# Attention over pooled keys, then a gated MLP: three chunks pooled partly by VectorE, and a re-planned order

## The chip, the cores and the metric

One core of one Trainium2 chip. The metric is device time of one execution in microseconds, median of the runs; a profiled execution is taken beside them.

## The reference

Four batches, each with 12288 queries of 128 channels and a 384 x 32 image of 128 channels. The image is averaged over 4 x 4 pixels, which leaves 768 positions, and multiplied with `w_sr`; the result is both keys and values. Softmax attention follows, and the output goes row by row through an MLP of width 2048.

```python
kv_pool = kv.reshape(B, H // r, r, W // r, r, C).mean(axis=(2, 4))      # r = 4
k = v = kv_pool.reshape(B, -1, C) @ w_sr
s = (q @ k.transpose(0, 2, 1)) / np.sqrt(C)
a = np.exp(s - s.max(-1, keepdims=True)); a /= a.sum(-1, keepdims=True) + 1e-09
x = (a @ v).reshape(B * S, D)
h = x @ w_in
out = (h * (1.0 / (1.0 + np.exp(-1.702 * h)))) @ w_out
```

Inputs and output are float32; the kernel computes its matmuls in bf16.

## The kernel before

The 49152 rows are 96 groups of 512 rows. A group has 6 attention chunks (128 keys each) and 16 MLP chunks (128 of the 2048 hidden columns each). A chunk is *filled* (one 512-column matmul into a PSUM bank), goes through ScalarE (exponential L359, gated unit L619) into a slot of the SBUF tile `ag`, and is *drained*: four 129-column matmuls per attention chunk (L370, the 129th column sums the weights), one 512-column matmul per MLP chunk (L627). Fills are done two or three chunks at a time in banks 0 to 2 and 3 to 5; ScalarE takes such a fill as one instruction. Drains accumulate in the remaining banks (6 and 7; with two-chunk fills also 2 and 5), handed out by `acc()`, and VectorE evacuates them: L393 and L396 for attention, L638 for the MLP. Order of the work: attention of groups 0 to 47 (batches 0 and 1), their MLP, attention of groups 48 to 95, their MLP.

Some chunks bypass ScalarE: VectorE computes the exponential (`early_exp`) or the gated unit (`lent_gelu`) of the chunks in `rolling`, `lent` and `early`, one instruction at a time between its other work (`early_step`).

Every engine works through its instructions in order, and the kernel writes that order itself (`manual_schedule`): a planner at the end of the file keeps a clock `now` for TensorE, `dve` for VectorE and `end` for ScalarE in units of a 512-column matmul, and emits a fill, a drain or one of the `extras` by these. Its constants (`COST`, `COPY`, `SMALL`, `PAUSE` and so on) and the lists `sizes`, `first`, `SUM`, `rolling`, `lent` decide the order; semaphores then keep the data right on the chip.

**Keys.** For batches 0 and 1 the image is loaded in six chunks of 128 image rows by 16 pixels x 128 channels (a half of the image's columns). `load_chunk` issues them on GpSimd's DMA queue, which casts to bf16 on the way, into slots of the tile `x` that attention output will fill later. `pool_chunk` sums the pixels on TensorE: 16 matmuls with the pixel as the weights and `sum4` (128 x 32) as the moving operand (L141); L144 copies the result, and `key_and_value` makes keys and values (L163 to L166). Batch 1's loads are issued at groups 10 and 12 behind a `gate` (a VectorE and a GpSimd memset that hold the queue back until then), and their pooling at the groups in `SUM`. For batches 2 and 3 the sums are made by accumulating DMAs into `kvs` during the first MLP (`add_kv`, L175), `sum_kv` (L181), `put_pooled`, `turn_pooled` and `make_k`, each step some groups after the last (`background_moe`).

**Queries.** Groups 0 to 9 are loaded by casting DMAs on GpSimd's queue (`load_q`) and turned on TensorE (`transpose_q`, L244). Groups 6 and 7 share one load, `load_q(1, 2, 4)`, issued after the six chunks of batch 0. For 6 to 9 `later` puts the transposes in `extras` at the step in `first`. All others go through `cast_q`, a DRAM copy in bf16, and a transposing DMA on SP's queue (`load_qT`).

Of the kernel before, what the change touches and what calls it, by code (L numbers as in the profile page):

```python
# [24 lines left out]
def kernel(  # L25
    ctx, tc, q, kv, w_sr, moe_w_in, moe_w_out, out,
):
    nc = tc.nc
    B, N, C = q.shape
    _, H, W, _ = kv.shape  # L30
    r = 4
    Hp, Wp = H // r, W // r
    J = Hp * Wp
    JC = J // 128
    d_ff = moe_w_in.shape[1]
    FCH = d_ff // 128
    scale = 1.0 / (C ** 0.5)
    G = 512
    SG = 4 * G
    NG = B * N // G  # L40
    NS = NG // 4
    GB = NG // B
# [18 lines left out]
    R = 2  # L61
    XS = NS // R
    EARLY = 4
    AG = 102

    cpool = ctx.enter_context(tc.tile_pool(name="const", bufs=1))
# [46 lines left out]
    def x_tile(s):  # L113
        return x[:, s % XS * SG:(s % XS + 1) * SG]
# [2 lines left out]

    HC = H // 128
    h = J // 2
    kv_tiles, kv_sums, pooled, pTs, kTs, vs = {}, {}, {}, {}, {}, {}  # L120

    def new_keys(b):
        kTs[b] = kvres.tile([128, J], BF, name="kT")
# [4 lines left out]
    def load_chunk(b, jc):  # L128

        a, ch = divmod(jc, HC)  # L130
        t = x_tile(XS - 1 - jc)
        nc.gpsimd.dma_start(out=t, in_=kv_r[b, a, ch])
        kv_tiles[b, jc] = t.rearrange("p (wp w1 c) -> p w1 wp c", w1=r, c=C)

    def pool_chunk(b, jc):

        ps = acc()
        t = kv_tiles.pop((b, jc))
        for wp in (0, 2, 1, 3) if (b, jc) == (0, 0) else range(4):
            for w in range(r):  # L140
                nc.tensor.matmul(ps[:, 32 * wp:32 * wp + 32], t[:, w, wp, :], sum4,  # L141
                                 start=(w == 0), stop=(w == r - 1))
        pTs[b, jc] = kvtmp.tile([128, 128], BF, name="pTc", bufs=2)
        nc.vector.tensor_copy(pTs[b, jc], ps[:, 0:128])  # L144

# [24 lines left out]
    def add_kv(b, n):  # L170
        i, w = divmod(n, r)
        if n == 0:
            kv_sums[b] = kvsum.tile([Hp, 2, Wp, C], F32, name="kvs")
        for i2 in range(2):
            nc.gpsimd.dma_start(out=kv_sums[b][:, i2], in_=kv_p[b, i, w, :, i2],  # L175
                                **({"accum_op": ADD} if n else {}))
# [7 lines left out]
        nc.sync.dma_start(out=pool_bf[b, a].rearrange("w h c -> h w c"), in_=pooled[b, a])  # L184

    def turn_pooled(b, a):
        pTs[b, a] = kvtmp.tile([128, 1, h], BF, name="pT")
        nc.sync.dma_start_transpose(out=pTs[b, a], in_=pool_bf[b, a].rearrange("w h c -> (w h) c"))

    def put_k(b, a):  # L190
# [60 lines left out]

    first_f = x[:, 0:2 * SG].bitcast(F32)
    nc.sync.dma_start(out=first_f, in_=kv_r[0, 0, 0])
    w_sr_f = cpool.tile([128, C], F32)
    nc.sync.dma_start(out=w_sr_f, in_=w_sr)
    load_q(0, 0, 1)
    load_q(0, 1, 2)
# [22 lines left out]
    for m in range(0, 128, 32):  # L280
        p = slice(m, m + 32)
# [19 lines left out]
            nc.tensor.matmul(banks[:32, 2, :], ones, ones.unsqueeze(1).broadcast_to([128, 16, 32]),  # L301
                             start=True, stop=True)

    w_in_sb = cpool.tile([128, d_ff], BF)
    w_out_sb = cpool.tile([128, FCH, C], BF)

    ag = agpool.tile([128, AG, 512], BF, name="ag")
    warm(13)
# [26 lines left out]
        return K * len(free_frames())  # L335

    early = range(NG // R, NG // R + EARLY)
    rolling = [(i, JC - 1) for i in (31, 35, 45, 55, 56, 63, 64, 78, 91)]
    lent = [(g, FCH - 1) for g in (4, 6, 8, 9, 13, 15, 17, 53, 54, 56, 58, 60, 64, 65, 68, 69, 72, 73, 77, 81, 83, 85, 88, 91, 93)]
    turn = [("a",) + c for c in rolling if c[0] < early[0]] + [("m",) + c for c in lent if c[0] < early[0]]  # L340
    turn += [("a",) + c for c in rolling if c[0] > early[-1]] + [("m",) + c for c in lent if c[0] > early[-1]]
    aside = agpool.tile([128, K, 512], BF, name="aside")
# [10 lines left out]

    def fill_attn(chunks, ps):
        for k, (i, jc) in enumerate(chunks):
            rhs = qTs[i // 4][:, 0, (i % 4) * G:(i % 4 + 1) * G]
            nc.tensor.matmul(ps[:, k, :], kTs[i // GB][:, jc * 128:(jc + 1) * 128], rhs,  # L357
                             start=True, stop=True)
        nc.scalar.activation(place([("a",) + c for c in chunks]), ps, AF.Exp, scale=scale)  # L359
# [68 lines left out]
        raw = qpool.tile([128, 1, SG], BF, name="qT")[:, 0, 0:2 * G].bitcast(F32)  # L428

    def early_step():  # L430
        nonlocal steps
        on_dve(next(steps))
        if steps.gi_frame.f_locals["last"]:
            steps = None
            made[early_todo.pop(0)] = dve

    def early_exp(ps, out):
        last = False
# [49 lines left out]
        yield 3.5  # L488

    raw = None  # L490
    made, used = {}, []
    steps, early_todo = None, [c for c in rolling if c[0] < early[0]]
    early_todo += [c for c in lent if c[0] < early[0]]
    early_todo += [(i, jc) for i in early for jc in range(JC)]
# [38 lines left out]
        nc.gpsimd.memset(one, 0.0)  # L533

    TURN = {6: 3, 7: 4, 8: 5, 20: 6, 21: 7, 22: 8, 25: 9, 32: 10, 35: 11, 42: 12}
    SUM = {13: (0,), 14: (1,), 15: (2,), 17: (3,), 19: (4,), 22: (5,)}
    CAST = {0: [5], 13: [6], 14: [7], 15: [8], 16: [9], 26: [10, 11], 27: [12]}
    CAST_MOE = {20: 13, 21: 14, 22: 15, 23: 16, 33: 17, 34: 18, 35: 19, 36: 20, 37: 21, 38: 22, 39: 23}

    def background(i):  # L540

        first_round = i < GB * 2
        s = TURN.get(i, NS) if first_round else i // 4 + 3 if i % 4 == 0 else NS
        if s < NS:
            load_qT(s)
        if i == 5:
            load_rest(2, 2)
        if i in CAST:
            gate()
            for s in CAST[i]:  # L550
                cast_q(s)
        if i in (10, 12):
            gate()
            for jc in range(i % 10 * 3 // 2, i % 10 * 3 // 2 + 3):
                load_chunk(1, jc)
        for jc in SUM.get(i, ()):
            extras.extend([(pool_chunk, 1, jc), (key_and_value, 1, jc)])
        if i in (28, 33, 38):
            put_away(0, (i - 28) // 5)
        if i in (31, 36, 41):  # L560
            bring_back(0, (i - 31) // 5)
        if i == 40:
            new_raw()
        if i == 28:
            gate()
            nc.gpsimd.dma_start(out=w_in_sb, in_=moe_w_in)
        if i == 29:
            gate()
            nc.gpsimd.dma_start(out=w_out_sb, in_=moe_w_out.rearrange("(o p) c -> p o c", p=128))

    def background_moe(g):

        n, g = divmod(g, 4 * XS)
        m, odd = divmod(g - 9, 2)
        m += FIRST
        if n == 0 and FIRST <= m < RT // PART:
            (bring_back if odd else put_away)(n, m)
        g += n * 4 * XS
        nonlocal low, raw
        if g == 12:  # L580
            low = EARLY * JC
            order[:] = [f for f in order if f >= low // K]
        if g in CAST_MOE:
            gate()
            cast_q(CAST_MOE[g])
        if g in (41, 42):
            load_qT(g - 28)
        if g == 43:
            raw = None
            background(early[0])  # L590
        for b, lo in ((2, 0), (3, 24)):
            if lo <= g < lo + 8:
                gate()
                add_kv(b, g - lo)
            for a in range(2):
                step = g - lo - 9 - a
                if step == 0:
                    sum_kv(b, a)
                    on_dve(3.5)
                    put_pooled(b, a)  # L600
                if step == 2:
                    turn_pooled(b, a)
                if step == 4:
                    extras.append((make_k, b, a))
# [63 lines left out]


    NA, NM = NG * JC, NG * FCH  # L670
    chunks, sizes = [], [1] * 2 + [2] * 26
    chunks += [(0, 0), (1, 0), (0, 1), (1, 1)]
    chunks += [(i, jc) for i in range(2, 6) for jc in range(2)]
    chunks += [(i, jc) for jc in range(2, JC) for i in range(6)]
# [57 lines left out]
    def prepare(p):  # L732
# [3 lines left out]
        for i, jc in part:  # L736
# [20 lines left out]
        12: [(pool_chunk, 0, 4)],  # L757
        13: [(key_and_value, 0, 4)],
        15: [(pool_chunk, 0, 5)],
        16: [(key_and_value, 0, 5), (later, 6)],  # L760
        17: [(later, 7)],
        18: [(later, 8), (later, 9)]}

    FIXED, CHUNK, SWITCH, HANDOVER, EVACUATE = 0.295, 1.978, 6.0, 1.0, 4.5
    COST = {pool_chunk: (1.9, 2.6), key_chunk: (0.3, 2.4), value_chunk: (0.3, 2.4),
            transpose_q: (1.05, 4.2), early_fill: (1.0, 5.5), key_and_value: (0.55, 3.5),
            make_k: (0.8, 3.2)}  # L770
    COPY = {pool_chunk: 1.5, key_chunk: 1.5, value_chunk: 1.5, key_and_value: 2.8, transpose_q: 3.2}
    SMALL = 0.26
    RECIPROCAL = 8.2
    PAUSE = 1.0
    end, extra_at = [], 0.0
    source, dve = None, 0.0
    early_left = 2 * (G // T) * EARLY
# [1 line left out]
    def on_dve(cost):  # L779
        nonlocal dve  # L780
        dve = max(dve, now + 1.0) + cost
# [36 lines left out]
    for n in range(len(seq)):  # L818
        fill(n + 2)
        jobs(n + 3)  # L820
        while True:
# [3 lines left out]
            f = None  # L825
            if extras and now >= max(extra_at, bank):
                f, *args = extras[0]
            if steps and dve <= now + 3.0:
                early_step()
            near = todo and todo[0][0] == "m" and todo[0][2] > 10  # L830
# [4 lines left out]
            if f:  # L835
                now = max(now, bank) + COST[f][0]
                f(*args)
                free[last_acc] = dve + 1.0 if f is early_fill else copied(f)
                if f is make_k:
                    on_dve(2.5)  # L840
                extra_at = max(now + PAUSE, dve + 1.5 if f is make_k else 0.0)
                if f is early_fill:
                    pass
                else:
                    extras.pop(0)
                continue
# [67 lines left out]
```

## Time and profile before

| What | us |
|---|---|
| median of 3 runs (lowest, highest) | 946.6 (946.47, 946.94) |
| profiled execution, device time | 946.45 |
| its span in the profile | 944.7 |
| TensorE matmuls busy | 938.5 |
| ScalarE busy | 930.5 |
| VectorE busy | 655.5 |
| GpSimd busy | 66.7 |

PE is TensorE's matmuls, PEld its weight loads, DVE VectorE, ACT ScalarE, POOL GpSimd, SP the engine that issues most DMAs. Times inside the profile count from the span's start. Ends of matmuls are modelled, so starts are compared where gaps matter. The granted clock of TensorE was 1.0 throughout. The two attention stages lie at about 8 to 160 us and 483 to 640 us.

### The profile page before, as it was taken

What the parts mean: (1) busy time and instruction counts of PE and PEld (TensorE: products, weight loads), DVE (VectorE), ACT (ScalarE), POOL (GpSimd) and SP (SyncE); (2) the same over time, 40 slices, a digit from 0 to 9 for tenths busy, and PEclk for the clock granted to TensorE, in tenths of its full rate; (3) what the DMA queues carried; (4) which work ended last, traced back from release to release, by engine and by line L of the source; (5) the groups of instructions that cost most, each with busy time, mean ns of one, the idle gap of its engine ahead of it and who ended that gap; (6) DMA issues with size and microseconds to landing.
All of it is one profiled execution on the core that took longest, in us unless ns stands there. A gap on an engine that the chain in (4) does not pass through costs nothing.

```text
span 944.7 us, 15547 instructions
## 1 busy us (share of the span) xinstructions
PE 938.5 (99%) x6278; PEld 500.9 (53%) x6278; DVE 655.5 (69%) x1202; ACT 930.5 (98%) x706; POOL 66.7 (7%) x115
## 2 busy tenths in 40 slices
PE   9999999999999999999999999999999999999998
PEld 4777776444444444445446777744444444444444
DVE  5547565896878789878757645458777986386681
ACT  6999999999999999999999999999999999999997
POOL 3101003310000332000000000000000000000000
PEclk9999999999999999999999999999999999999999
DMA  9998947996877899664435683652222221212222
GB/s 210 206 196 176 189 90 102 145 134 139 167 151 115 123 144 130 116 111 93 63 63 117 131 157 91 116 124 41 38 38 41 37 42 34 44 34 45 34 45 45
DMA packets 380456, 97.30 MB, mean 103 GB/s; under 512 B 354560, under 2 KB 377984, under 8 KB 379904
## 3 DMA queue, kind: packets, MB, share of 16 engines
q1 hardware_dynamic: 351840, 64.19, 36.9%
q0 software_dynamic: 28272, 31.99, 22.3%
q8 instruction: 49, 0.80, 0.4%
q14 instruction: 23, 0.19, 0.1%
q10 hardware_dynamic: 272, 0.13, 0.0%
HBM read 52.49 MB, written 49.81 MB: 108 GB/s over the span
## 4 chain that ended last, share of the span: by engine, by line
PE 98%; DMA 1%; ACT 0%; DVE 0%; POOL 0%; issue 0%; POOLq 0%
PE banks L627 35%; PE banks L617 35%; PE banks L370 14%; PE banks L357 12%; PE banks L422 1%; DMA x<-in_kv_dram 1%; PE banks L416 1%; PE banks L141 0%; ACT ag L359 0%; PE banks L655 0%; POOL x L230 0%; PE banks L163 0%; PE banks L301 0%; PE banks L244 0%; PE banks L203 0%
## 5 line engine op out<-in xcount | busy, mean ns | idle before, releaser
L619 ACT ACTIVATE ag<-banks 128x1536 bf16<-128x1536 f32 (+1 forms) x507 | 677.7, 1468 | 0.0
L617 PE MATMUL banks<-x,w_in_sb 128*128 128x512 bf16 x1511 | 408.8, 379 | 0.0
L627 PE MATMUL banks<-ag,w_out_sb 128*128 128x512 bf16 x1495 | 405.2, 379 | 0.0
L359 ACT ACTIVATE ag<-banks 128x1536 bf16<-128x1536 f32 (+2 forms) x191 | 245.9, 1410 | 3.3 <-PE banks L357 2.9
L627 PEld LDWEIGHTS <-w_out_sb 128*128 128x128 bf16 x1520 | 148.5, 98 | 178.2
L617 PEld LDWEIGHTS <-w_in_sb 128*128 128x128 bf16 x1511 | 146.5, 98 | 170.6 <-issue 0.5
L370 PEld LDWEIGHTS <-ag 128*128 128x128 bf16 x2268 | 145.7, 98 | 44.3 <-issue 0.5
L370 PE MATMUL banks<-v,ag 128*128 128x129 bf16 x2268 | 163.6, 220 | 0.1
L357 PE MATMUL banks<-qT,kT 128*128 128x512 bf16 x543 | 148.4, 379 | 1.3 <-DVE kT L165 0.4
L638 DVE STREAM_TRANSPOSE o_sb<-banks 128x512 f32<-128x512 f32 x95 | 67.3, 708 | 79.8 <-PE banks L627 79.0
L453 DVE SCALAR_TENSOR_TENSOR ea<-ea,eb 128x512 f32<-128x512 f32 x132 | 90.5, 686 | 4.1 <-DVE ea L453 0.6
L393 DVE RECIPROCAL rec<-banks 128x3 f32<-128x3 f32 x124 | 22.2, 179 | 92.7 <-PE banks L370 92.2
L484 DVE RECIPROCAL eb<-ea 128x256 f32<-128x256 f32 x50 | 84.9, 1726 | 0.9
L396 DVE TENSOR_TENSOR x<-banks,rec 128x384 bf16<-128x384 f32 x124 | 69.1, 557 | 4.3
L477 DVE SCALAR_TENSOR_TENSOR ea<-ea,eb 128x512 f32<-128x512 f32 x100 | 68.3, 683 | 2.7
L357 PEld LDWEIGHTS <-kT 128*128 128x128 bf16 x543 | 45.9, 98 | 26.0 <-issue 1.4
L175 POOL DMA_DIRECT2D kvs<-in_kv_dram x32 | 40.7, 1338 | 20.8 <-DMA kvs<-in_kv_dram 17.5
L442 DVE TENSOR_SCALAR ea<-banks 128x512 f32<-128x512 f32 x33 | 22.8, 692 | 26.0 <-PE banks L422 25.7
L464 DVE TENSOR_SCALAR qT<-banks 128x512 f32<-128x512 f32 x25 | 17.3, 692 | 34.0 <-PE banks L416 34.0
L533 POOL MEMSET gate_tile<- 1x1 f32 x38 | 3.6, 94 | 320.4 <-DVE gate_tile L532 315.1
L448 DVE SCALAR_TENSOR_TENSOR eb<-eb,ea 128x512 f32<-128x512 f32 x33 | 22.8, 691 | 0.9
L472 DVE SCALAR_TENSOR_TENSOR eb<-eb,ea 128x512 f32<-128x512 f32 x25 | 17.3, 692 | 0.9
(78 smaller groups left out, 316.7 us busy)
## 6 DMA issues: line engine op xcount, KB each, us to landing
out_dram<-o_sb SPq DMA_DIRECT2D x380, 64.0 KB, 1.9
kvs<-in_kv_dram POOLq DMA_DIRECT2D x32, 384.0 KB, 6.4
q_bf<-in_q_dram POOLq DMA_DIRECT2D x21, 512.0 KB, 7.0
x_bf<-x SPq DMA_DIRECT2D x13, 768.0 KB, 5.6
x<-in_kv_dram POOLq DMA_DIRECT2D x11, 512.0 KB, 10.2
x_bf<-x SPq DMA_DIRECT2D x6, 384.0 KB, 4.7
x<-in_kv_dram SPq DMA_DIRECT2D x1, 1024.0 KB, 5.1
x<-in_q_dram POOLq DMA_DIRECT2D x4, 256.0 KB, 12.1
```

The costliest lines, as they stand in the source:

```text
L175: nc.gpsimd.dma_start(out=kv_sums[b][:, i2], in_=kv_p[b, i, w, :, i2], **({"accum_op": ADD} if n else {}))
L357: nc.tensor.matmul(ps[:, k, :], kTs[i // GB][:, jc * 128:(jc + 1) * 128], rhs, start=True, stop=True)
L359: nc.scalar.activation(place([("a",) + c for c in chunks]), ps, AF.Exp, scale=scale)
L370: nc.tensor.matmul(av_of[u][:, k * (C + 1):(k + 1) * (C + 1)], weights(("a", i, jc))[:, o:o + T], vs[i // GB][:, jc, 0:C + 1], start=(jc = ...
L396: nc.vector.tensor_tensor(to, ps[:, :, 0:C], rec.unsqueeze(2).broadcast_to([128, TS, C]), MUL)
L453: nc.vector.scalar_tensor_tensor(a, a, COEFFS[k], b, ADD, MUL)
L477: nc.vector.scalar_tensor_tensor(a, a, COEFFS[k], b, ADD, MUL)
L484: nc.vector.reciprocal(b[:, m:m + 256], a[:, m:m + 256])
L617: nc.tensor.matmul(ps[:, k, :], w_in_sb[:, fc * 128:(fc + 1) * 128], x[:, g % (4 * XS) * G:(g % (4 * XS) + 1) * G], start=True, stop=True)
L619: nc.scalar.activation(place([("m",) + c for c in chunks]), ps, AF.Gelu_apprx_sigmoid)
L627: nc.tensor.matmul(o_of[g], w_out_sb[:, fc, :], weights(("m", g, fc)), start=(fc == 0), stop=(fc == FCH - 1))
L638: nc.vector.transpose(o_sb, o_of.pop(g))
```

## The change

- Chunks 1, 3 and 4 of batch 1 (`ADDED`) are loaded as float32, without the cast, into memory that is free at that time: `kvs`, the tile of both MLP weights, and two slots of `x`. `kvs` also takes the place of the float32 copy of `w_sr`.
- `add_row` adds the four pixels of a row on VectorE, in three instructions, the last one giving bf16; `pool_added` then needs 4 matmuls in place of 16.
- Planner constants, `rolling`, `lent`, `SUM` and `first` get other values: two-chunk fills go on for 47 fills in place of 26, the transposes of groups 6 to 9 come at other steps, `lent` has 26 chunks in place of 25.
- The second half of the sums of batches 2 and 3 comes one group later, and turned keys get two buffers.

Across the whole program TensorE has 36 matmuls fewer, ScalarE six instructions more.

```diff
+    ADDED = (1, 3, 4)
...
+    kvs = kvsum.tile([128, 2, Wp, C], F32, name="kvs")
+    w_both = cpool.tile([128, 2 * d_ff], BF, name="w_both")
+    homes = [kvs.rearrange("p a w c -> p (a w c)"), w_both.bitcast(F32)]
+    homes += [x[:, s * SG:(s + 2) * SG].bitcast(F32) for s in (XS - 6, XS - 4, XS - 2)]
+    wide = dict(zip(ADDED, homes))
+    plain = [jc for jc in range(JC) if jc not in wide]
+    spots = {jc: XS - 1 - (JC if len(wide) == JC - 1 else k) for k, jc in enumerate(plain)}
...
-        t = x_tile(XS - 1 - jc)
+        if b and jc in wide:
+            nc.gpsimd.dma_start(out=wide[jc], in_=kv_r[b, a, ch])
+            return
+        t = x_tile(spots[jc] if b else XS - 1 - jc)
...
+    def add_row(jc):
+
+        last, wp = False, None
+        t = wide[jc].rearrange("p (wp e) -> p wp e", wp=r)
+        narrow_sum = wide[jc].bitcast(BF).rearrange("p (wp e) -> p wp e", wp=r)[:, :, 4 * C:5 * C]
+        for m in (0, 2):
+            nc.vector.tensor_tensor(t[:, m:m + 2, 0:2 * C], t[:, m:m + 2, 0:2 * C], t[:, m:m + 2, 2 * C:4 * C], ADD)
+            yield 3.2
+        nc.vector.tensor_tensor(narrow_sum, t[:, :, 0:C], t[:, :, C:2 * C], ADD)
+        added[jc] = narrow_sum
+        extras.extend([(pool_added, 1, jc), (key_and_value, 1, jc)])
+        last = True
+        yield 3.3
+
+    def pool_added(b, jc):
+
+        ps = acc()
+        t = added.pop(jc)
+        for wp in range(r):
+            nc.tensor.matmul(ps[:, 32 * wp:32 * wp + 32], t[:, wp, :], sum4, start=True, stop=True)
         pTs[b, jc] = kvtmp.tile([128, 128], BF, name="pTc", bufs=2)
         nc.vector.tensor_copy(pTs[b, jc], ps[:, 0:128])
...
-        pTs[b, a] = kvtmp.tile([128, 1, h], BF, name="pT")
+        pTs[b, a] = kvtmp.tile([128, 1, h], BF, name="pT", bufs=2)
...
-    w_sr_f = cpool.tile([128, C], F32)
+    w_sr_f = kvs[:, 0, 0, :]
...
-    rolling = [(i, JC - 1) for i in (31, 35, 45, 55, 56, 63, 64, 78, 91)]
-    lent = [(g, FCH - 1) for g in (4, 6, 8, 9, 13, 15, 17, 53, 54, 56, 58, 60, 64, 65, 68, 69, 72, 73, 77, 81, 83, 85, 88, 91, 93)]
+    rolling = [(i, JC - 1) for i in (33, 36, 45, 53, 56, 62, 76, 89, 92)]
+    lent = [(g, FCH - 1) for g in (6, 7, 10, 13, 14, 17, 52, 53, 55, 58, 59, 62, 63, 67, 68, 71, 73, 75, 77, 78, 82, 83, 86, 88, 91, 92)]
...
-    SUM = {13: (0,), 14: (1,), 15: (2,), 17: (3,), 19: (4,), 22: (5,)}
+    SUM = {13: (0,), 14: (1,), 15: (2,), 17: (3,), 21: (4,), 22: (5,)}
...
         for jc in SUM.get(i, ()):
-            extras.extend([(pool_chunk, 1, jc), (key_and_value, 1, jc)])
+            if jc in wide:
+                sums.append(add_row(jc))
+            else:
+                extras.extend([(pool_chunk, 1, jc), (key_and_value, 1, jc)])
...
-                step = g - lo - 9 - a
+                step = g - lo - 9 - 2 * a
...
-    chunks, sizes = [], [1] * 2 + [2] * 26
+    chunks, sizes = [], [1] * 2 + [2] * 47
...
         15: [(pool_chunk, 0, 5)],
-        16: [(key_and_value, 0, 5), (later, 6)],
-        17: [(later, 7)],
-        18: [(later, 8), (later, 9)]}
+        14: [(later, 6)],
+        15: [(pool_chunk, 0, 5), (later, 7)],
+        16: [(key_and_value, 0, 5)],
+        17: [(later, 8)],
+        26: [(later, 9)]}
...
-    COST = {pool_chunk: (1.9, 2.6), key_chunk: (0.3, 2.4), value_chunk: (0.3, 2.4),
+    COST = {pool_chunk: (2.1, 2.6), pool_added: (0.55, 2.6), key_chunk: (0.3, 2.4), value_chunk: (0.3, 2.4),
...
-    COPY = {pool_chunk: 1.5, key_chunk: 1.5, value_chunk: 1.5, key_and_value: 2.8, transpose_q: 3.2}
-    SMALL = 0.26
+    COPY = {pool_chunk: 1.5, pool_added: 1.5, key_chunk: 1.5, value_chunk: 1.5, key_and_value: 2.8, transpose_q: 3.2, make_k: 2.9}
+    SMALL = 0.2647
...
-    PAUSE = 1.0
+    PAUSE = 2.0
...
+            if sums and not steps:
+                steps = sums.pop(0)
             if steps and dve <= now + 3.0:
                 early_step()
...
-                if f is make_k:
-                    on_dve(2.5)
```

The key 15 stands twice in `first` after the change; the second one, with both entries, counts.

More of the change, by code (lines that the diff above doesn't have):

```diff
@@ L119 @@
     h = J // 2
-    kv_tiles, kv_sums, pooled, pTs, kTs, vs = {}, {}, {}, {}, {}, {}
+    kv_tiles, kv_sums, pooled, pTs, kTs, vs, added = {}, {}, {}, {}, {}, {}, {}
+    kvs = kvsum.tile([128, 2, Wp, C], F32, name="kvs")
[5 more added lines that the diff above has]
+    spots = {jc: XS - 1 - (JC if len(wide) == JC - 1 else k) for k, jc in enumerate(plain)}
     def new_keys(b):
@@ L142, in pool_chunk @@
                                  start=(w == 0), stop=(w == r - 1))
+        pTs[b, jc] = kvtmp.tile([128, 128], BF, name="pTc", bufs=2)
+        nc.vector.tensor_copy(pTs[b, jc], ps[:, 0:128])
+    def add_row(jc):
[15 more added lines that the diff above has]
+            nc.tensor.matmul(ps[:, 32 * wp:32 * wp + 32], t[:, wp, :], sum4, start=True, stop=True)
         pTs[b, jc] = kvtmp.tile([128, 128], BF, name="pTc", bufs=2)
@@ L172, in add_kv @@
         if n == 0:
-            kv_sums[b] = kvsum.tile([Hp, 2, Wp, C], F32, name="kvs")
+            kv_sums[b] = kvs[0:Hp]
         for i2 in range(2):
@@ L302, in warm @@
                              start=True, stop=True)
-    w_in_sb = cpool.tile([128, d_ff], BF)
-    w_out_sb = cpool.tile([128, FCH, C], BF)
+    w_in_sb = w_both[:, 0:d_ff]
+    w_out_sb = w_both[:, d_ff:2 * d_ff].rearrange("p (o c) -> p o c", c=C)
     ag = agpool.tile([128, AG, 512], BF, name="ag")
@@ L355, in fill_attn @@
         for k, (i, jc) in enumerate(chunks):
+            assert i < GB or (i // GB, jc) in vs
             rhs = qTs[i // 4][:, 0, (i % 4) * G:(i % 4 + 1) * G]
@@ L430, in early_step @@
     def early_step():
-        nonlocal steps
+        nonlocal steps, extra_at
         on_dve(next(steps))
         if steps.gi_frame.f_locals["last"]:
+            if "wp" in steps.gi_frame.f_locals:
+                extra_at = max(extra_at, dve + 1.0)
+            else:
+                made[early_todo.pop(0)] = dve
             steps = None
-            made[early_todo.pop(0)] = dve
     def early_exp(ps, out):
@@ L490 @@
     raw = None
-    made, used = {}, []
+    made, used, sums = {}, [], []
     steps, early_todo = None, [c for c in rolling if c[0] < early[0]]
@@ L556, in background @@
         for jc in SUM.get(i, ()):
-            extras.extend([(pool_chunk, 1, jc), (key_and_value, 1, jc)])
+            if jc in wide:
+                sums.append(add_row(jc))
+            else:
+                extras.extend([(pool_chunk, 1, jc), (key_and_value, 1, jc)])
         if i in (28, 33, 38):
```

## The prediction

> **What bounds the kernel now.** The page was read first: busy shares, then the chain that ended last.
>
> ```profile
> PE 938.5 (99%) x6278; PEld 500.9 (53%) x6278; DVE 655.5 (69%) x1202; ACT 930.5 (98%) x706; POOL 66.7 (7%) x115
> PE 98%; DMA 1%; ACT 0%; DVE 0%; POOL 0%; issue 0%; POOLq 0%
> ```
>
> The first row is each engine's busy us, share and instructions; the second, the chain's shares. TensorE and ScalarE both look full, but the chain runs over TensorE alone. A modelled busy share hides short gaps, so I took the starts of all 6278 matmuls from the trace. Back to back, a 512-column matmul takes 216 ns, one of 128 or 129 columns 56, of 32 columns 25. Against these floors TensorE loses only 7.2 us from its first matmul (0.97 us) to its last (940.95 us): 3.0 before 12.5 us, 3.5 from there to 65.4 us, 0.7 in the other 875. So the time is a sum of matmuls, plus waits in the first 65 us. ScalarE starts a three-chunk exponential every 1.33 us at best and averages 1.35: there is about 1% of slack, and ScalarE does not set the end. VectorE is free a third of the time. The windows by stage say the same: the start, then chunks of batch 1, then the steady second stage.
>
> ```profile
> 12.00:27.00 15.00, 13.93 (x164) 8.56 (x163) 9.03 (x24) 14.49 (x16) 1.56 (x4) 1.00 1.13 223
> 27.00:47.00 20.00, 20.00 (x224) 14.50 (x223) 11.26 (x34) 20.00 (x19) 3.48 (x10) 1.00 1.10 199
> 47.00:77.00 30.00, 29.88 (x387) 21.70 (x386) 13.23 (x49) 30.00 (x23) 2.17 (x7) 1.00 1.01 194
> ```
>
> The columns are busy us of TensorE, weight loads, VectorE, ScalarE and GpSimd, then granted clock (1.00), DMA share and GB/s. Only the start has TensorE below full, and there DMA is saturated (share above 1).
>
> **What is removed.** Three chunks are pooled by 4 matmuls in place of 16: 36 fewer. A window on one pooling shows the price.
>
> ```profile
> 20.59:20.99 0.40, 0.40 (x17) 0.40 (x17) 0.33 (x1) 0.40 (x2) 0.00 (x0) 1.00 1.06 215
> ```
>
> The group of its weight loads lists 96 ns for one:
>
> ```profile
> L141 PEld LDWEIGHTS <-x 128*128 128x128 bf16 x192 | 6.3, 96 | 4.2 <-DMA x<-in_kv_dram 1.4 <-DVE x L291 0.8 <-issue 0.2
> ```
>
> Sixteen matmuls and their loads take 0.40 us, 25 ns a pair: the loads overlap. 36 x 25 ns = 0.90 us, all on the path: **-0.9**. Laying the rows at these intervals along both instruction orders gives 930.04 us of TensorE work before and 929.14 after; the rest of its program is the same work in another order.
>
> The Trainium skill ("TensorE: Matmul & The Clock Gate", LDWEIGHTS) puts a 128-column weight load at columns / 1.2, some 107 ns; by that, 36 would save an estimated 3.8 us. The windowed row, with 25 ns, disagrees.
>
> **What is added off the path.** Each wide chunk has two adds over 512 elements per partition and a third over 512 with a bf16 result. Nearest row: L181, 676 ns for 96x512. 9 x 0.68 = 6.1 us of VectorE, spread over 20 us where it now works about half the time (11.26 of 20.00, 13.23 of 30.00). In the new order they stand between the drains' reciprocal and multiply (0.18 + 0.56 us a drain); from the first add to the pooled copy after it, VectorE has 4.6 us of work for 5.2 us of TensorE's. Cover is the spare accumulator banks: four while fills are two chunks wide, two later, each about 1 us of drain. I take 0; if the cover fails, one add, 0.7 us, per chunk, at most 2.
>
> Two-chunk fills go on for 21 fills more, in place of 14 of three: 21 x 904 - 14 x 1330 ns = +0.4 us of ScalarE (starts 904 and 1330 ns apart when back to back). One more second-matmul chunk goes to VectorE (-0.44 us of ScalarE, about 11 us of VectorE in a stage where it is busy 31 of 40). With ScalarE's 1% of slack: 0 on the path.
>
> Second buffer for turned keys, the second half of the sums one group later: VectorE's wait of 3.7 us at L181 goes, of which nobody waited on TensorE (two of its gaps there, 0.1 each): 0. On SP the second half's DMAs (put_pooled, turn_pooled, put_k, turn_k) move past one group's four output DMAs; three output buffers cover 20 us. 0. The changed constants only order the emission.
>
> **The loads.** Chunks 1, 3 and 4 now write 1 MB each instead of 0.5, from GpSimd's queue, and the chunks behind them and the four casts of q queue behind those. Before, successive casting loads landed 2.3 to 2.5 us apart (45.41, 47.69, 50.13 us). No row shows an uncast 1 MB load on this queue. Low bound: the same, as both read 1 MB. High bound: kvs loads of 384 KB f32, which land 1.5 us apart when quiet and up to 3.4 us when busy, 4 to 9 us per MB. I take 2.45: its source reads are the same and its rows as long, where the kvs rows have 512-byte pieces. Then, with the wait of the next part, the loads start near 41.6 us; chunk 0 lands near 47.3 (5.7 us, as before) and is pooled near 48.9, chunk 1 lands near 49.7 and VectorE reaches its add near 52.0, chunk 3 near 54.6 for 59.2: 0.
>
> **The transposes of raw q, moved forward: the one wait on the path.** The new order puts group 6's transposes (L244) ahead of chunk 5's pooling, group 7's just behind it. Their data is one cast load, issued at 7.56 us.
>
> ```profile
> 7.56 0.70 POOL L230 DMA_DIRECT2D x<-in_q_dram  x1
> ```
>
> From issue to landing:
>
> ```profile
> x<-in_q_dram POOLq DMA_DIRECT2D x1, 256.0 KB, 16.8
> ```
>
> And TensorE's timeline of before around its use (start, us, line, tiles, count, and idle time with its releaser):
>
> ```profile
> 19.65 0.67 PE L370 MATMUL banks<-v,ag 128*128 128x129 bf16 x9
> ...
> 23.57 0.56 PE L141 MATMUL banks<-sum,x 128*128 128x32 bf16 x16
> ...
> 24.61 0.39 PE L244 MATMUL banks<-ident,x 128*128 128x128 bf16 x4
> ...
> 26.88 0.59 PE L357 MATMUL banks<-qT,kT 128*128 128x512 bf16 x2 [0.23 <-ACT ag L359]
> ```
>
> The load lands at 24.31 us, at the saturated queues' pace (neighbours at 23.05 and 25.55), and its transposes begin at 24.61, so it was just in time. Up to the drain at 19.65 the two orders are alike. From there the changed one has, before group 6, six fills (1.30 us), 15 drains (0.84), 16 pooling (0.40) and two key/value matmuls (0.11): 2.65 us, and about 0.3 of waits like those of before (chunk 4 lands at 20.52). It arrives at 22.6 us and waits until 24.36: **+1.75**. Queued behind are drains, fills and chunk 5's pooling; ScalarE, without a fill, idles about 1.6 us.
>
> What that wait swallows: between 24.61 and 77 us TensorE of before waited 1.6 us (0.40 at 26.4 for ScalarE, 0.33 at 33 to 36, 0.27 at 48.9, 0.18 at 65, small ones). Those for ScalarE come back, as ScalarE is delayed too: I keep 0.35 around 28 us, 0.2 in the two-chunk stretch and 0.4 at the passage to three. So **-0.65** (between 0 and -1.6). After 77 us: unchanged.
>
> Sum: -0.90 + 1.75 - 0.65 = +0.2 us. The profiled execution took 946.45 us (span 944.7), 0.15 below the median of 946.6. So 946.65 for it, **946.8 us** for the median. This kernel's measurement tells about 0.2% (1.9 us) from no change.
>
> **The rivals.**
>
> *Slower, by late wide loads.* If an uncast load takes over about 4.7 us, chunk 1 comes later than VectorE reaches its add, and everything behind it on VectorE's queue waits: drains' evacuations, so banks, so TensorE. At the busy kvs price (8 us) VectorE waits 3.3 us for chunk 1 and 6.6 for chunk 3; less about 2.5 and 2 us that the banks cover, TensorE loses 0.8 + 4.6: 952 us. For it: DMA share is 1.0 to 1.1 there. Against: 4 us when quiet, and longer rows. 0.13. Other late copies, banks or chains on VectorE in the new order, each under 1 us but adding to over 2: 0.15, 948.5 to 950.
>
> The Trainium skill ("DMA: Bandwidth & Descriptors", Where 436 GB/s comes from) caps the SBUF side at 435 GB/s, an estimated 2.4 us per MB, so uncast would land like cast; no run yet shows it.
>
> *Faster, because weight loads are exposed.* If each removed pair costs its listed load, 96 ns, 36 save 3.5 us, not 0.9: 944.2. Against it, the sixteen in 0.40 us. 0.04. It is what the Trainium skill's rule on loads above would bring.
>
> *Faster, because the early wait absorbs more.* All 1.6 us of old waits vanish, and two or three later ones: -0.9 + 1.75 - 2.7 = -1.9 at the very best, 944.7. For it: no wait after 77 us matters. Against: ScalarE is starved by the same wait. 0.06.
>
> **How the numbers follow.** No measurable change 0.62 (own range 945.3 to 948.4), faster 0.10, slower 0.28. The range reaches from -1.3 (all old waits gone) to +2.5 or so (two adds uncovered plus one lost bank): 945.3 to 949.2; it leaves out the late loads at full price and the exposed weight loads.
>
> **What would show it.** Right: a wait of 1.5 to 2 us at L244's transposes ending near 24.4 us, TensorE full after it, pooling of wide chunks in 0.10 us, no wait on VectorE for wide chunks. Wrong: group 6's data landing before 23 us (then about 945), VectorE waiting for DMA at the adds, or TensorE gaps after 80 us above 1 us.

## The result, and the profile after

The changed kernel takes 949.16 us (949.02 to 949.36), the kernel before in the same comparison 946.76 (946.47 to 947.05): ratio 1.0026, 95% interval 1.0017 to 1.0034. That is 2.4 us slower, where 946.8 was forecast; it lies just inside the stated range, whose top was 949.2. The profiled execution took 949.02 us with a span of 947.2, against 946.45 and 944.7.

The page of the changed kernel, busy shares and the chain that ended last:

```profile
PE 932.2 (98%) x6128; PEld 500.5 (53%) x6242; DVE 667.4 (70%) x1226; ACT 929.3 (98%) x712; POOL 66.7 (7%) x115
PE 94%; DMA 2%; ACT 2%; issue 1%; DVE 0%; POOL 0%; POOLq 0%
```

TensorE's matmul count is 150 lower, but its weight loads, 36 fewer, tell the change: 114 matmul records are missing from this trace, which also lowers the busy time. The chain now holds DMA and ScalarE with 2% each, where DMA had 1% and ScalarE 0%. The windows of the first stages show where TensorE is less busy (TensorE, weight loads, VectorE, ScalarE, GpSimd, clock, DMA share, GB/s):

```profile
12.00:27.00 15.00, 12.05 (x147) 7.41 (x149) 8.09 (x22) 13.15 (x14) 1.56 (x4) 1.00 1.13 223
27.00:47.00 20.00, 19.51 (x220) 14.48 (x224) 11.27 (x34) 19.83 (x23) 2.60 (x7) 1.00 1.03 175
47.00:77.00 30.00, 29.47 (x349) 21.53 (x354) 18.41 (x58) 30.00 (x27) 3.13 (x10) 1.00 1.01 255
```

The first window falls from 13.93 to 12.05 us. Missing records lower these sums too (220 matmuls to 224 loads in the second row, 349 to 354 in the third), so the waits are read from starts below. TensorE's timeline in the first window names the wait:

```profile
20.48 0.56 PE L152 MATMUL banks<-sum,x 128*128 128x32 bf16 x16
...
21.61 0.50 PE L405 MATMUL banks<-v,ag 128*128 128x129 bf16 x6
22.15 0.39 PE L392 MATMUL banks<-qT,kT 128*128 128x512 bf16 x1
24.26 0.40 PE L278 MATMUL banks<-ident,x 128*128 128x128 bf16 x4 [1.72 <-DMA x<-in_q_dram]
...
26.90 0.60 PE L392 MATMUL banks<-qT,kT 128*128 128x512 bf16 x2 [0.31 <-DVE kT L199]
...
28.62 0.59 PE L392 MATMUL banks<-qT,kT 128*128 128x512 bf16 x2 [0.33 <-ACT ag L394]
```

Group 6's transposes (L278 here, L244 before) are reached behind the fill of 22.15, and their load lands at 24.21 us. The two later brackets are a wait for key evacuation and one for ScalarE, which had no fill in the meantime. The view of waits from 20 to 70 us has both waits, TensorE's for the load and ScalarE's for a fill (us in total, times, longest):

```profile
PE banks L278 <- DMA x<-in_q_dram: 1.7, 1, 1.7
ACT ag L394 <- PE banks L392: 1.6, 2, 1.5
```

The load lands in 16 parts, each with a time in the trace. Fifteen had landed by 23.34 us; the last came 0.87 us later, and the transposes need it. Why one part is late is taken up below, under the instruction fetches.

**Where the 2.5 us are.** Modelled ends hide short gaps, so all matmul starts of a trace are laid along the kernel's own matmul order at back-to-back intervals (215.85 ns for 512 columns, 56.5 for 129, 56 for 128, 25.1 for 32, 163 for 384). Where a matmul's record is missing, its weight load, whose record is there, gives its place. What a start lies behind that sum is TensorE's time "lost so far". The orders sum to 930.67 us before and 929.77 after.

```
lost so far (us) at    22.5     25     80    480    640   last matmul   then to the span's end
before                 7.86   7.96   9.43   9.83  10.28      10.33          3.73
after                  7.82   9.50  11.21  11.94  12.94      13.41          4.12
e1_first_old           7.73   7.84   9.26  10.02  10.94      11.41          4.29
e4_old_plan            7.79   7.90  10.39  11.56  12.84      13.36          3.94
e7_plan_only           7.81   7.91   9.87  11.08  12.23      12.93          4.08
e10_sizes26            7.89   7.99  10.54  11.86  13.61      14.15          4.36
```

From the first two rows, after against before: -0.90 for the order; -0.04 up to 22.5 us; +1.58 at the transposes (1.68 lost there, 0.10 before); +0.24 from 25 to 80 us; +0.88 from 80 to 640 us; +0.42 in the last group; +0.39 behind the last matmul. The sum is +2.57, the spans differ by 2.5.

**The tail.** The timeline of the last group, after and then before:

```profile
939.14 0.67 PE L696 MATMUL banks<-w_both,ag 128*128 128x128 bf16 x9
939.34 0.72 DVE L679 STREAM_TRANSPOSE o_sb<-banks 128x512 f32<-128x512 f32 x1 [4.93 <-PE banks L668]
940.11 3.23 PE L696 MATMUL banks<-w_both,ag 128*128 128x128 bf16 x55 [0.31 <-DVE o_sb L679]
```

```profile
936.96 0.33 PE L655 MATMUL banks<-w_out_sb,ag 128*128 128x128 bf16 x3
...
937.16 0.72 DVE L638 STREAM_TRANSPOSE o_sb<-banks 128x512 f32<-128x512 f32 x1 [5.81 <-PE banks L627]
937.56 3.60 PE L655 MATMUL banks<-w_out_sb,ag 128*128 128x128 bf16 x61
```

One of the last group's four accumulators lies in the bank of the group before it, which VectorE empties first (the row of L679, L638 before). After, TensorE comes to it with no other work left and loses 0.47 us against the intervals (the bracket shows 0.31 of it); before, a fill and drains stood in between.

### The profile page after: what moved, and what is told of

It is laid out like the page before. It is cut to its first block, busy times and chain, and to the rows that moved or that the text cites. A ratio compares the mean times of both kernels' runs of the same rounds, so it can differ in the third digit from the quotient of the medians.

```text
span 947.2 us, 15391 instructions
## 1 busy us (share of the span) xinstructions
PE 932.2 (98%) x6128; PEld 500.5 (53%) x6242; DVE 667.4 (70%) x1226; ACT 929.3 (98%) x712; POOL 66.7 (7%) x115
## 4 chain that ended last, share of the span: by engine, by line
PE 94%; DMA 2%; ACT 2%; issue 1%; DVE 0%; POOL 0%; POOLq 0%
PE banks L668 34%; PE banks L658 34%; PE banks L405 13%; PE banks L392 11%; DMA x<-in_q_dram 2%; ACT ag L394 2%; PE banks L457 1%; PE banks L451 1%; PE banks L696 0%; PE banks L237 0%; PE banks L152 0%; DVE o_sb L679 0%; PE banks L278 0%; DVE qT L284 0%; DVE x L431 0%
## 5 line engine op out<-in xcount | busy, mean ns | idle before, releaser
L658 PE MATMUL banks<-x,w_both 128*128 128x512 bf16 x1477 | 404.2, 379 | 1.6
L668 PE MATMUL banks<-ag,w_both 128*128 128x512 bf16 x1459 | 401.6, 379 | 1.9
L394 ACT ACTIVATE ag<-banks 128x1536 bf16<-128x1536 f32 (+2 forms) x198 | 245.6, 1454 | 4.9 <-PE banks L392 2.3
L668 PEld LDWEIGHTS <-w_both 128*128 128x128 bf16 x1520 | 148.6, 98 | 179.2 <-issue 0.2
L658 PEld LDWEIGHTS <-w_both 128*128 128x128 bf16 x1510 | 146.5, 98 | 170.3 <-issue 0.5
L392 PE MATMUL banks<-qT,kT 128*128 128x512 bf16 x498 | 145.4, 379 | 3.7 <-DVE kT L199 0.7
L679 DVE STREAM_TRANSPOSE o_sb<-banks 128x512 f32<-128x512 f32 x95 | 66.9, 704 | 72.4 <-PE banks L668 71.9
L491 DVE SCALAR_TENSOR_TENSOR ea<-ea,eb 128x512 f32<-128x512 f32 x132 | 90.6, 686 | 3.2
L522 DVE RECIPROCAL eb<-ea 128x256 f32<-128x256 f32 x52 | 88.2, 1725 | 0.9
L515 DVE SCALAR_TENSOR_TENSOR ea<-ea,eb 128x512 f32<-128x512 f32 x104 | 71.1, 683 | 2.8
L392 PEld LDWEIGHTS <-kT 128*128 128x128 bf16 x543 | 46.2, 97 | 24.9 <-issue 1.7
L486 DVE SCALAR_TENSOR_TENSOR eb<-eb,ea 128x512 f32<-128x512 f32 x33 | 22.8, 691 | 1.0
L517 DVE SCALAR_TENSOR_TENSOR ea<-ea,ee 128x512 f32<-128x512 f32 x26 | 18.0, 692 | 0.9
```

Of the source, the lines that this page charges most:

```text
L491: nc.vector.scalar_tensor_tensor(a, a, COEFFS[k], b, ADD, MUL)
L515: nc.vector.scalar_tensor_tensor(a, a, COEFFS[k], b, ADD, MUL)
L522: nc.vector.reciprocal(b[:, m:m + 256], a[:, m:m + 256])
L658: nc.tensor.matmul(ps[:, k, :], w_in_sb[:, fc * 128:(fc + 1) * 128], x[:, g % (4 * XS) * G:(g % (4 * XS) + 1) * G], start=True, stop=True)
L668: nc.tensor.matmul(o_of[g], w_out_sb[:, fc, :], weights(("m", g, fc)), start=(fc == 0), stop=(fc == FCH - 1))
L679: nc.vector.transpose(o_sb, o_of.pop(g))
```

## The experiments

The theories: (A) the early wait is one cost, and the later waits come from the order in their own stages; (B) the later waits follow from the early one. For the later ones: ScalarE is late (Z), a planner constant (S) or the lists `rolling` and `lent` (L) place the work badly, or the wide chunks and their two-chunk fills do it. Beside these runs the kernel before took 946.6 to 946.8 us.

**Transposes as before.**

```diff
-        14: [(later, 6)],
-        15: [(pool_chunk, 0, 5), (later, 7)],
-        16: [(key_and_value, 0, 5)],
-        17: [(later, 8)],
-        26: [(later, 9)]}
+        16: [(key_and_value, 0, 5), (later, 6)],
+        17: [(later, 7)],
+        18: [(later, 8), (later, 9)]}
```

> The changed kernel (949.16 us) with the steps of batch 0's last chunk and of the raw-q transposes as before: groups 6 to 9 turned after chunk 5's pooling. Theory A, the 1.9 us wait for group 6's data is the main loss and what follows is independent of it: the wait goes, 0.3 to 0.5 of ordinary waits of that stretch stay, 947.4 to 947.8. Rival B, the later waits for ScalarE (0.9 us after 77 us) are a consequence of ScalarE idling in that wait: they go too, 946.5 to 946.9. Rival C, the wide loads or VectorE's adds cost the time: 948.8 to 949.2.

947.27 us, ratio 1.0006 (0.9997 to 1.0016). TensorE's timeline at the same place:

```profile
24.44 0.22 PE L198 MATMUL banks<-w_sr_sb,pTc 128*128 128x128 bf16 x1
24.49 0.39 PE L278 MATMUL banks<-ident,x 128*128 128x128 bf16 x4
```

No bracket: the wait is gone, and 1.9 us with it. In the table its row stays 1.9 to 2.0 us below the changed kernel's from 80 us to the last matmul, so the later waits are as they were: A holds, B falls. The other 0.65 us against before is theirs and the tail's.

**The load earlier instead.** The load of groups 6 and 7 is issued ahead of chunk 5's.

```diff
+        if jc == JC - 1:
+            load_q(1, 2, 4)
...
-    load_q(1, 2, 4)
```

> The changed kernel with only the load of groups 6 and 7 put before the load of chunk 5 on GpSimd's queue; TensorE's order is the changed one. Group 6's data should land near 21.7 us, chunk 5 near 24.2 in place of 23.0. Theory A: no wait at the transposes, 0.6 to 0.9 us at chunk 5's pooling instead, so 1.0 to 1.3 us gained: 947.9 to 948.2. Rival B: some of the later waits go as well, 947.4 to 947.8. Rival C: no gain, 949.1.

948.28 us, ratio 1.0017 (1.0008 to 1.0026). The transposes no longer wait; chunk 5's pooling does:

```profile
24.72 0.57 PE L152 MATMUL banks<-sum,x 128*128 128x32 bf16 x16 [0.67 <-DMA x<-in_kv_dram]
```

From 22.5 to 25 us TensorE lost 1.07 us in place of 1.68. The time came down by 0.9, a little less than expected. The profiled execution took 948.68, 0.4 above the median, so its rows need not show all of the gain.

**The tail's order.** The held accumulator's first matmuls come behind hidden chunk 6 instead of 2.

```diff
-        parts = [(m, fc) for m in range(4) if m != held or fc > 2]
-        if fc == 2:
-            parts += [(held, f) for f in range(3)]
+        parts = [(m, fc) for m in range(4) if m != held or fc > 6]
+        if fc == 6:
+            parts += [(held, f) for f in range(7)]
```

(and the same bounds in the loop over `f`)

> The changed kernel with the last group's matmuls reordered: the accumulator in the bank that group 94 still holds starts after hidden chunk 6 and not after chunk 2. Theory: the wait of 0.47 us at 939.6 us is for VectorE's evacuation (L679) of that bank; 18 matmuls of 56 ns come before it and the wait falls under 0.1, 948.7 us. Rival: the gap is a missing record or another wait, 949.1 to 949.2.

949.12 us, ratio 1.0027 (1.0016 to 1.0037): no gain, so the forecast missed. The timeline shows the wait gone, all 64 matmuls in one row:

```profile
939.21 3.74 PE L696 MATMUL banks<-w_both,ag 128*128 128x128 bf16 x64
```

The last matmul came 0.39 us earlier, but the last output landed 3.28 us behind it, where it was 2.56 after and 2.38 before. What is known of that is below. This profiled execution took 949.34, 0.2 above its median.

**The mechanism with the old lists.** `rolling`, `lent`, `SUM`, `first`, the fill sizes, `SMALL`, `PAUSE`, pooling's cost and the step of the second half as before; three wide chunks stay.

> The mechanism alone: wide chunks, adds on VectorE, shared tiles and two buffers, but lists, constants and steps of before (two-chunk fills end as before, SMALL 0.26, PAUSE 1, rolling, lent, SUM and first of before, second half of the sums one group after the first). Theory A: 36 matmuls of 25 ns less and no new wait in the start, plus about 0.4 at the end, where its last drains follow each other without a fill as in the changed kernel: 946.0 to 946.5. Rival C, loads or adds cost: 947.5 and more.

948.8 us, ratio 1.0024 (1.0014 to 1.0033), above the forecast. Without the early wait (7.90 at 25 us) it loses 2.49 us from 25 to 80, where before lost 1.47, and 2.45 from 80 to 640, where before lost 0.85. That is where its rival, a cost of the loads or the adds, had put it. Planner hooks, shared tiles and second buffers aside, this kernel differs from the one before by the wide chunks alone, so with 26 two-chunk fills these, or what they do to the order, do bring waits. The next runs ask whether that holds with 47.

**The plan without the mechanism.** From e1: `ADDED = ()`, so all chunks are cast and pooled by 16 matmuls.

> The kernel of e1 without wide chunks: all six of batch 1's chunks cast on load and pooled by 16 matmuls, everything else of e1 kept. Theory: the wide chunks are worth their 36 matmuls, 0.9 us, and nothing else, so 948.0 to 948.4. Rival: the adds on VectorE or the 1 MB loads cost something that the plan hides, so the kernel without them is no slower, 947.0 to 947.5.

949.5 us, ratio 1.0029 (1.0018 to 1.004). It is 2.2 us above e1, where 0.9 of matmuls come back; the rest is waits (1.96 from 25 to 80 us, 2.36 from 80 to 640; 1.42 and 1.68 in e1). So with 47 two-chunk fills, taking the wide chunks out gains nothing. It also changes the order of the work, for which the constants were not laid out.

**Single parts of the plan**, each one line from e1. `SMALL = 0.26`:

> The kernel of e1 with one planner constant, SMALL, back from 0.2647 to 0.26. Theory S: the larger value makes the planner hold TensorE back against ScalarE, which is where the waits of about 20 ns per fill after 77 us come from; then the waits from 77 to 160 us and from 480 to 640 us (1.0 and 0.9 us in e1) fall by half or more, 946.3 to 946.8. Rival: they come from the lists of chunks given to VectorE or from the longer stretch of two-chunk fills, 947.1 to 947.5.

947.43 us, ratio 1.0007 (0.9997 to 1.0016): the waits only moved (1.07 us between 60 and 80, 0.20 from 80 to 160, 0.94 from 480 to 640). `rolling` and `lent` of before:

> The kernel of e1 (947.27 us) with rolling and lent, the lists of chunks that VectorE takes over from ScalarE, as before the change. Theory L: the later waits (0.7 us from 77 to 160 us, 0.9 from 480 to 640) are ScalarE's, because the new lists relieve it later; with the old lists each falls to 0.5 or less, 946.2 to 946.7. Rival: the longer stretch of two-chunk fills, or the order itself, 947.1 and more.

948.8 us, ratio 1.0021 (1.0012 to 1.0031): slower than e1, so the new lists, put back by themselves, are not the fault; S and L fall in the form that was tested. Two-chunk fills ending after 26:

> The kernel of e1 with two-chunk fills ending after 26 as before. Theory Z: the 21 further two-chunk fills cost ScalarE 0.4 us, so that it limits TensorE from 77 to 160 us; the waits there fall by 0.3 to 0.5 us, those from 480 to 640 us stay: 946.8 to 947.0 at best, if the pooling of batch 1 with two banks in place of four does not give it back. Rival: the four banks are what lets the pooling go without waits, so the waits from 45 to 77 us grow by 0.3 to 1.0 us: 947.3 to 948.2.

949.74 us, ratio 1.0033 (1.002 to 1.0045). It loses 2.55 us from 25 to 80 us, against 1.42 in e1, and 3.07 from 80 to 640, against 1.68. e4, with the same 26 fills, lost 2.49 from 25 to 80; the kernel before, with 26 and no wide chunks, lost 1.47. That two-chunk fills leave more accumulator banks for the time in which VectorE adds is the reading; the runs show only that the shorter series costs 2.5 us.

**Five wide chunks**, `ADDED = (1, 2, 3, 4, 5)`, with e3's tail:

> The kernel of e1 with five wide chunks (1 to 5) in place of three and with the reordered end of e3. 24 matmuls fewer again (0.6 us) and no wait of 0.47 us at the end; the last instruction fetch moves past the last matmul. Theory: 946.2 to 946.8 if the stores are not held by it, 946.8 to 947.3 if they are. Rival: VectorE, with 4.1 us more of adds, delays evacuations and TensorE waits for banks: 948 and more.

948.85 us, ratio 1.0022 (1.0013 to 1.0031). The order sums to 929.16 us, 0.6 below e1's, but TensorE lost 2.9 us from 47 to 80 us. Its timeline has waits for ScalarE and key evacuation there:

```profile
75.20 0.81 PE L392 MATMUL banks<-qT,kT 128*128 128x512 bf16 x3 [0.44 <-ACT ag L394]
...
78.95 0.39 PE L392 MATMUL banks<-qT,kT 128*128 128x512 bf16 x1 [0.33 <-DVE kT L199]
```

**The end: instruction fetches.** The DMA view from 940 to 948 us, of e1:

```profile
q8 instruction: 1, 0.02, 0.9%
...
out_dram<-o_sb ACTq DMA_DIRECT2D x1, 128.0 KB, 2.3
out_dram<-o_sb SPq DMA_DIRECT2D x1, 128.0 KB, 2.2
```

and of the kernel before:

```profile
out_dram<-o_sb ACTq DMA_DIRECT2D x1, 128.0 KB, 1.9
out_dram<-o_sb SPq DMA_DIRECT2D x1, 128.0 KB, 1.8
```

The traces of these kernels have 49 such fetches of 16 KB, one about every 130 of TensorE's matmuls with their loads; e11, with 60 matmuls fewer than before, has 48. They come at the same place in TensorE's order: number 48 begins at weight load 6101 in the kernel before and in the changed one. The last one begins 1.81 us ahead of the last matmul before, 0.48 after, 0.30 in e1. With 36 pairs fewer the fetches fall elsewhere, and the last now runs beside the last stores, which land later: 2.56 us behind the last matmul after and 2.73 in e1, 2.38 before. The test gives TensorE 36 pairs more at the start, by splitting the 13 warming matmuls into 49:

```diff
-    warm(13)
+    for k in range(49):
+        cols = 5 if k % 7 < 2 else 4
+        nc.tensor.matmul(banks[:32, 2, 0:32 * cols], ones, ones.unsqueeze(1).broadcast_to([128, cols, 32]),
+                         start=True, stop=True)
```

> The kernel of e1 (947.27 us) with the 13 warming matmuls at the start replaced by 49 shorter ones of about the same total time, so that TensorE has as many instructions as before. Theory: the last 16 KB instruction fetch, which came 0.3 us before the last matmul in e1 and 1.8 us before it in the kernel before, goes back to about 1.8 us, and the last output stores land 0.3 to 0.5 us sooner after the last matmul: 946.8 to 947.0. Rival: the fetch only happens to lie there and the end stays, 947.2 to 947.4.

948.04 us, ratio 1.0016 (1.0006 to 1.0025). At the end it came as expected: last fetch 1.85 us ahead, landings back to

```profile
out_dram<-o_sb ACTq DMA_DIRECT2D x1, 128.0 KB, 1.8
out_dram<-o_sb SPq DMA_DIRECT2D x1, 128.0 KB, 1.8
```

But the first fetch moved too, from 17.7 to 13.45 us, ahead of more of the saturated loads of the start, and the chunk pooled next came late (L395 is L392 of the changed kernel):

```profile
14.15 0.59 PE L395 MATMUL banks<-qT,kT 128*128 128x512 bf16 x2
15.67 0.57 PE L152 MATMUL banks<-sum,x 128*128 128x32 bf16 x16 [0.93 <-DMA x<-in_kv_dram]
```

In e1 that pooling starts at 14.67, without a wait. Fifteen of the load's 16 parts had landed by 14.61 in e1 and 14.66 in e5, the last at 14.62 and 15.62. So e5 lost 0.7 us at the start. The same with e3's tail:

> e5 with the last group's matmuls reordered as in e3, where the wait of 0.47 us went but the time stayed because the last stores landed later. Theory: with the fetch out of the way the 0.4 us show, 946.3 to 946.6. Rival: the stores' own queue sets the end, 946.8 to 947.0.

947.45 us, ratio 1.001 (1.0 to 1.0019): 0.6 under e5. The 946.3 to 946.6 that were expected did not reckon with e5's loss at the start. (The profiled execution, 948.37, lies 0.9 above the median and had lost 0.56 us more than e5's by 20 us.) The last group lost 0.03 us and the last output landed 2.39 us behind the last matmul: with the fetch out of the way, the tail's 0.4 us can be had.

All 14 traces agree on the landing. In the four whose last fetch begins 1.8 us or more ahead of the last matmul (before, e5, e8, e11), the last output lands 2.38 to 2.39 us behind that matmul. In the other ten the fetch begins 1.2 us ahead or later, and it lands 2.51 to 3.28 us behind. In nine of these ten, fifteen of the last store's 16 parts land within 2.6 us, and one part lands 0.1 to 0.6 us behind them; in the four no part is more than 0.03 us late. The tenth is e3. Its last store also took longer to issue, e3 and then the changed kernel:

```profile
943.30 0.96 SPq L707 DMA_DIRECT2D out_dram<-o_sb  x1
```

```profile
943.70 0.39 SPq L707 DMA_DIRECT2D out_dram<-o_sb  x1
```

Why it did is open; e8 and e11 have the same tail and 0.39.

The early wait hangs on a fetch too. The first one begins at 17.8 us in the changed kernel, and the next three loads to land (20.44, 22.95 and 24.21 us, the last that of groups 6 and 7) each have one part 0.8 to 0.9 us behind the other fifteen; the two before them have none. In e5, with the fetch at 13.45, the late parts begin two loads earlier (15.62 and 17.94). So, by an estimate from these times, some 0.9 of the 1.7 us waited at the transposes is the fetch's; no run took the fetch away from that wait.

**The later waits: ScalarE.** From e1, with the same order of instructions; exponentials of the second attention stage shorter by 16 of 512 columns.

```diff
-        nc.scalar.activation(place([("a",) + c for c in chunks]), ps, AF.Exp, scale=scale)
+        to = place([("a",) + c for c in chunks])
+        if chunks[0][0] >= GB * 2:
+            to, ps = to[:, :, 0:G - 16], ps[:, :, 0:G - 16]
+        nc.scalar.activation(to, ps, AF.Exp, scale=scale)
```

> The kernel of e1 (947.27 us), same instruction order on every engine, but in the second attention stage (480 to 640 us) each exponential of ScalarE covers 496 of 512 columns of a chunk, which leaves out 3% of the exponentials there and makes such an instruction about 40 ns shorter. Theory Z: the waits of about 20 ns before fills in that stage (0.9 us in e1, 0.45 before the change) are TensorE waiting for ScalarE; they fall to 0.3 or less, 946.5 to 946.8. Rival: they come from VectorE or from banks; they stay, 947.2 to 947.4.

946.86 us, ratio 1.0003 (0.9993 to 1.0012). ScalarE's groups by shape, the three-chunk exponentials of the second stage and of the first (L397 is L394 of the changed kernel):

```profile
L397 ACT ACTIVATE ag<-banks 128x1488 bf16<-128x1488 f32 x86 | 114.6, 1413 | 0.4
L397 ACT ACTIVATE ag<-banks 128x1536 bf16<-128x1536 f32 x63 | 84.7, 1604 | 0.0
```

From 480 to 640 us TensorE lost 0.35 us in place of e1's 0.92, and of the waits in front of fills and drains one of 0.107 us is left. From 80 to 160 us, where nothing was shortened, it lost 0.72 as in e1. So TensorE waits for ScalarE in that stage (Z), mostly 20 to 50 ns at a time.

None of these was faster than the kernel before; of those that do the whole work, e1 comes nearest.

## Why the prediction was wrong, step by step

- **36 matmuls fewer, -0.9:** right. Wide pooling takes about 0.10 us from its start to the next matmul's, on the timeline:

```profile
56.73 0.26 PE L176 MATMUL banks<-sum,kvs 128*128 128x32 bf16 x4
56.84 0.33 PE L405 MATMUL banks<-v,ag 128*128 128x129 bf16 x3
```

  At 25 ns a pair the account above closes to 0.1 us; exposed loads at 96 ns would leave 2.6 us of gain that no part of it shows. The Trainium skill ("TensorE: Matmul & The Clock Gate", LDWEIGHTS), with its 107 ns a load, gives a load's own length, which the trace lists as 96; the path pays the 25 ns of a pair, so the prediction's estimate of 3.8 us from it does not hold here.
- **VectorE's adds, 0.68 us each and hidden:** right. The first two and the third of chunk 1, by shape, with no wait:

```profile
L163 DVE TENSOR_TENSOR kvs<-kvs 128x512 f32<-128x512 f32 x2 | 1.3, 685 | 0.0
L165 DVE TENSOR_TENSOR kvs<-kvs 128x512 bf16<-128x512 f32 x1 | 0.7, 681 | 0.0
```

  VectorE reached the first at 52.43 us (52.0 forecast). e7 shows that taking the wide chunks out of this order gains nothing; in the orders with 26 two-chunk fills (e4, e10) TensorE lost 1.0 to 1.1 us more from 25 to 80 us than in the kernel before.
- **Uncast loads at 2.45 us:** right. Chunk 0 (cast) landed at 47.65, chunk 1 (uncast) at 50.16, chunk 2 (cast) at 52.58; chunk 3 at 56.31 and chunk 4 at 58.78, both uncast. Of these last two, fifteen of 16 parts had landed by 55.04 and 57.52, the last part 1.3 us later. One MB in 2.5 us either way. The Trainium skill ("DMA: Bandwidth & Descriptors", Where 436 GB/s comes from) has the ceiling of 435 GB/s; the trace of the uncast loads agrees, with 1.05 MB in 2.47 us, some 425 GB/s.
- **The wait at group 6's transposes, +1.75:** right, 1.68 us, or 1.58 against before; TensorE was ready for them at 22.6 us, as forecast. e1 takes it out, e2 takes 0.6 of it.
- **"What that wait swallows", -0.65:** this step failed. From 25 to 80 us the changed kernel lost 1.71 us, the kernel before 1.47. The old waits were not paid for by the early one. While TensorE waited, ScalarE waited 1.5 us for a fill, and TensorE then waited for ScalarE at 28.62 us; that this is why the others stayed as well is the reading. e1, without the early wait, lost 1.42 there. The prediction gave that argument against its rival and then deducted for it all the same.
- **"After 77 us: unchanged":** this step failed as well, by +0.88 up to 640 us. The prediction read ScalarE's 1% of slack as cover, but it is an average, which does not say where the slack lies. In this order ScalarE is a little late from 480 to 640 us (1.00 us lost there against 0.45 before; e12's shorter exponentials take 0.57 of e1's 0.92 away), and TensorE pays 20 to 50 ns in front of many fills, once 0.16. Each change of the plan moved these waits rather than removing them (e6, e9). Which decision of the planner makes ScalarE later there than in the order before stays open, as does the cause of the rest from 80 to 160 us (0.68 after, 0.19 before).
- **The end:** not in the prediction at all: +0.42 in the last group, +0.39 behind the last matmul. The first is a bank that VectorE has still to empty (e3 and e8 take it away). Of the second, 0.18 is the later landing (2.56 against 2.38), with the fetch moved beside the last stores; e5 moves it back and the landings follow. The other 0.21 lies behind the last landing, 1.56 us before the span's end in the changed kernel and 1.35 in the one before: VectorE's last closing instruction starts 1.21 us after the landing instead of 0.85. e5 leaves that as it was, and its cause is open.

The sum was +0.2; the failed deduction adds 0.9, the stages behind it 0.9, the end 0.8, and the start gave 0.2 back. The rival that gave 948.5 to 950 through several small waits was right in size and sign; its place, VectorE's queue at the wide chunks, was wrong. That the result lies inside the stated range is luck: its top was added up from two uncovered adds and a lost bank, and the time went elsewhere. One figure of the prediction does not come out again: it put what TensorE lost before the change at 7.2 us, and the table above gives 9.4 (10.33 less the first start at 0.97). Most of the difference lies in the first 12.5 us (4.6 in place of 3.0), and no term of its sum rests on it.

## What to carry to other kernels

In this kernel, whose bounding engine was full to within 1%, removed work came back as waits: the mechanism with the old lists (948.8) and the plan without the mechanism (949.5) were both slower than the two together (947.27). Before moving a step forward, set the landing time of its data against the time at which its engine will reach it; that gave +1.6 us of this result from one row of the trace. Do not credit an added wait with absorbing old ones when the engine that they wait for is starved by it too. Look at a load's last part and not only at its mean pace, and cost the last few us (banks, stores, fetches) as a stage of their own.

## What the runs showed of the hardware

TensorE's instructions arrive by DMA: 49 packets of 16 KB over the execution (48 in e11), one for about 130 matmuls with their loads, each taking 0.9 to 1.8 us. Their place depends on how many instructions went before. Behind a fetch in a saturated stage, one of the 16 parts of the loads that landed next came 0.8 to 1.3 us after the rest, and the load was waited for until that part. Thirty-six pairs more or fewer moved one further ahead in the saturated start, where the next chunk was waited for 0.93 us (e5), or beside the last stores, which then landed in 2.2 to 2.3 us instead of 1.8 to 1.9 (e1). In e3 the last output landed 3.28 us behind the last matmul, 0.9 later than before: 0.3 is the late part, and the rest goes with the longer issue of its store.
